# Turning k and x on VectorE in 32x32 blocks instead of on TensorE, with a new order table

## The chip, the cores and the metric

One core of one Trainium2 chip runs the whole program. The metric is device time in microseconds, the median of the runs. The engines are named as in the profile: PE (matmuls; PEld is its weight load), DVE (VectorE), ACT (ScalarE), POOL (GpSimd), and SP, which issues the DMAs.

## The reference

A recurrence with decay (RWKV style) over 4 samples, 8 heads, 768 steps, head size 48, and then a token mix and a feed-forward block of 384 to 1536 to 384 channels:

```python
for t in range(S):
    kt, vt, rt, wt = (k[:, :, t], v[:, :, t], r[:, :, t], w[:, :, t])
    cur = np.einsum('bhd,bhe->bhde', u[None] * kt, vt)
    y[:, :, t] = np.einsum('bhd,bhde->bhe', rt, state + cur)
    state = wt[:, :, :, None] * state + np.einsum('bhd,bhe->bhde', kt, vt)
...
h = xt @ U @ V                        # xt: channels by time, U and V of rank 32
u = x + h.transpose(0, 2, 1)
ch = np.maximum(u @ w_ch1, 0.0) @ w_ch2
return (u + ch).astype(np.float32)
```

## The kernel before

**Chunks.** Time is cut into chunks of 128 steps, six for a sample, 24 in all (chunk g = 6 x sample + chunk). A chunk lies on 128 partitions as channels (two heads of 48, at partitions 0 and 64) by 4 pairs of heads by 128 steps. Its work, with the step names that the order uses: loads of w, r with k, k and r once more in natural order, and v (LW, LRK, LKR, LV on SP); a pass over w that watches its range (GUARD on ACT); two scans of the decay (F and Q on DVE, a reciprocal R between them, the totals T); r and k scaled by them (RP, KS on DVE or POOL); the diagonal from r, k and u (RK, RU, RED) laid into a matrix (SEL, SEL2 on ACT or POOL); the scores (AM on PE) merged into that matrix (CP, a predicated copy on DVE); the output from within the chunk (YA on PE) and from the state (YZ on PE); the state's update (DS on PE; ZA and ZM add and decay it).

**Two turns.** DS contracts over time, so it needs the scaled k with time on partitions. PE turns it: KT, four transposes of 128x128 (L482) into a PSUM bank (tag tr), and ACT copies them to SBUF as kn (KN, L486). The last chunk of a sample updates no state, so 20 chunks are turned. The output y is copied to the tile xT, channels by time (XE, L598); the token mix contracts over time, so x is turned in the same way: XT, three transposes (L616), and XN on ACT (L620), for all 24 chunks. GA on PE takes xn.

**Token mix and feed-forward.** For a sample, GA, G4, SELM, GS and GSL make the rank-32 mix, HP adds it to x (UADD on DVE), and u is split into a high and a low half (UH, UL). Each half sample (384 steps) has twelve up groups of nine matmuls (UP b.h.f, L738; b the sample, h the half), each followed by HH (relu, ACT or DVE) and HL (the low half, DVE, L751), and three outputs of four down groups (DN b.h.c.part, L774), then O (DVE) and OUT (SP). UP, DN and HP share three PSUM buffers: HL, O or UADD frees one. The weights of the feed-forward are split early in the run by ACT, DVE and POOL.

**Order.** Every step is recorded first, then issued in the order of a written-out table (ORDER): a step's number, and whether it runs on its other engine (alt) and how many warming matmuls lead it. Each engine works off its own instructions strictly in that order, and waits on semaphores for the others. After the table's steps come a few rows that check that the decays stayed in range (per, cnt, low, flag); a scheduler puts them among the others, as soon as their inputs are there.

Of the kernel before, what the change touches and what calls it, by code (L numbers as in the profile page):

```python
# [37 lines left out]
def channel_order():
# [19 lines left out]
    "05J05f14y10V04b05L00r05+00Y04z04c05G14+06218Y08o05V00p10W06304-08P05K06001705g18y01905k05-"
    "00a01A00t05O05h11B00u00X15P06405w08x00v05005l08p01C05Q05100w06511y05R05M05p05N02x05S08Z15m06618R06E08Q00H05q"
    "05n08z00x06708T01D09F05r00J08a11+05s08U05t02z05o09E08V00K06801E00Z00L069i8b09N00M09O06A08q08c02N06B00N18d19h"  # L60
    "00b06C80O10c08r06D02y06F00d06G08s02+08+16H82-02P08W16I03008g46J09P08-"
    "06K08t03108h09019q06O06S08e09Q02E03206T08k4A709116P00e06L09R06M02W08u08l0AG06Q08f06N19g06U08m06R12G08i08v08n"
# [924 lines left out]
```

## Time and profile before

| | |
|---|---|
| median of 3 runs | 483.46 us (481.89 to 484.27) |
| profiled execution | 483.14 us, its span 481.4 us |
| mean granted clock of TensorE | 0.976 |
| PE, DVE, ACT, POOL busy | 449.4, 314.6, 171.2, 119.9 us |
| transposes of k on PE (L482) | 80, copies on ACT (L486) 20 of 594 ns |
| transposes of x on PE (L616) | 72, copies on ACT (L620) 24 of 487 ns |

The span runs from the first to the last instruction of the profiled execution; its own time is 1.7 us more. Shares of busy time are means over stages with different limits. Matmul and DVE records overlap with the next one of the same engine, so the time that an instruction takes of its engine is read from its start to the next start where the engine does not wait.

### The profile page before, as it was taken

Reading aid. Unit: us, or ns where it says so; the run is one execution under the profiler, and the core shown is the slowest. Engines: PE = TensorE matmul, PEld = TensorE weight load, DVE = VectorE, ACT = ScalarE, POOL = GpSimd, SP = SyncE. Lnnn points to the kernel's source line nnn. Section 1 sums busy time; section 2 is a strip of 40 time slices with the busy share of each in tenths; the row PEclk is TensorE's granted clock in tenths of the full one; section 3 lists DMA queues with packets and bytes.
Section 4 is the critical chain, followed back from the end, with each engine's and each line's share of the span. In section 5 each row is a group of like instructions: output and inputs, shape, how many; then the busy total and the mean of one; then the engine's idle time right before and its main releaser. Section 6 shows DMA issues by size and latency. Waiting matters only on the chain.

```text
span 481.4 us, 9783 instructions
## 1 busy us (share of the span) xinstructions
PE 449.4 (93%) x4041; PEld 409.8 (85%) x4041; DVE 314.6 (65%) x532; ACT 171.2 (36%) x446; POOL 119.9 (25%) x113
## 2 busy tenths in 40 slices
PE   7568797899999999999999999999999999999994
PEld 3357655799889889899999889799999899999994
DVE  8998999997999888967139558954134144422420
ACT  5485967874524532432044451320011121001000
POOL 3515422534643664402006050600000010000000
PEclk9786999999999999999999999999999999999999
DMA  8653867344105873214024360200000000000001
GB/s 301 226 193 93 298 212 252 116 146 157 38 23 154 251 216 90 75 43 130 18 83 149 100 218 34 84 20 1 33 18 0 19 17 18 0 34 16 1 17 39
DMA packets 20644, 47.38 MB, mean 98 GB/s; under 512 B 2480, under 2 KB 8880, under 8 KB 20592
## 3 DMA queue, kind: packets, MB, share of 16 engines
q1 hardware_dynamic: 20592, 46.67, 30.3%
q8 instruction: 34, 0.56, 0.5%
q14 instruction: 18, 0.15, 0.1%
HBM read 41.94 MB, written 4.72 MB: 97 GB/s over the span
## 4 chain that ended last, share of the span: by engine, by line
PE 70%; DVE 16%; DMA 5%; ACT 4%; issue 3%; POOL 1%; SPq 0%; ACTq 0%; DVEq 0%; POOLq 0%
PE f L774 29%; PE f L738 28%; PE aps L495 3%; DVE F L367 3%; DVE A L498 2%; DMA v<-in_vN 2%; PE y L555 2%; DVE cva_w L297 1%; DMA raw_w<-in_w 1%; PE trk L482 1%; DVE Q L380 1%; PE y L565 1%; PE trx L616 1%; DMA rk<-in_rkT 1%; DVE cva_w L283 1%
## 5 line engine op out<-in xcount | busy, mean ns | idle before, releaser
L738 PE MATMUL f<-u,w1h 128*128 128x384 f32 x576 | 157.0, 343 | 1.6 <-DVE u L705 0.8
L738 PEld LDWEIGHTS f<-u,w1h 128*128 128x128 f32 x576 | 105.3, 188 | 4.5 <-DVE u L705 1.5
L774 PE MATMUL f<-hh,w2h 128*128 128x384 f32 x288 | 99.4, 345 | 0.7 <-DVE hl L751 0.5
L774 PE MATMUL f<-hh,w2l 128*128 128x384 f32 x288 | 97.7, 339 | 0.7 <-POOL w2l L321 0.7
L738 PE MATMUL f<-u,w1l 128*128 128x384 f32 x288 | 97.5, 338 | 0.0
L751 DVE SCALAR_TENSOR_TENSOR hl<-f,hh 128x384 fp32r<-128x384 f32 x96 | 52.7, 552 | 34.9 <-ACT hh L745 33.7
L745 ACT ACTIVATE hh<-f 128x384 fp32r<-128x384 f32 x52 | 25.2, 486 | 137.6 <-PE f L738 137.5
L774 PE MATMUL f<-hl,w2h 128*128 128x384 f32 x288 | 66.7, 339 | 0.1
L774 PEld LDWEIGHTS f<-hh,w2h 128*128 128x128 f32 x288 | 54.1, 188 | 3.0 <-issue 1.0
L774 PEld LDWEIGHTS f<-hh,w2l 128*128 128x128 f32 x288 | 54.1, 188 | 1.2 <-POOL w2l L321 1.0
L738 PEld LDWEIGHTS f<-u,w1l 128*128 128x128 f32 x288 | 54.1, 188 | 0.0
L774 PEld LDWEIGHTS f<-hl,w2h 128*128 128x128 f32 x288 | 51.9, 188 | 0.5 <-DVE hl L751 0.4
L789 DVE TENSOR_TENSOR xT<-f,xT 128x384 f32<-128x384 f32 x24 | 13.3, 554 | 50.7 <-PE f L774 50.6
L747 DVE TENSOR_SCALAR hh<-f 128x384 fp32r<-128x384 f32 x44 | 24.2, 552 | 31.0 <-PE f L738 30.7
L430 ACT ACTIVATE A<-ident,dv 128x128 f32<-128x128 f32 x112 | 35.6, 392 | 24.8 <-PE y L565 16.1
L498 DVE COPY_PREDICATED A<-maskf,aps 128x1024 f32<-128x1024 uint32 x24 | 31.5, 1313 | 11.4 <-PE aps L495 5.7
L304 POOL TENSOR_TENSOR cva_w<-cva_w,raw_w 128x384 int32<-128x384 int32 x24 | 28.3, 1182 | 42.1 <-DVE cva_w L297 16.7
L432 POOL TENSOR_SCALAR_AFFINE_SELECT A<-dv 128x512 f32<-128x512 f32 x20 | 15.9, 804 | 75.5 <-PE y L565 58.9
L367 DVE TENSOR_TENSOR_SCAN F<-w,resets 128x517 f32<-128x517 f32 x24 | 33.4, 1399 | 1.8 <-POOL rk L392 1.3
L495 PE MATMUL aps<-rk 48*128 48x128 f32 x384 | 29.7, 297 | 3.8 <-DVE A L498 2.9
L380 DVE TENSOR_TENSOR_SCAN Q<-w,qd 128x516 f32<-128x516 f32 x24 | 32.5, 1354 | 0.1
L495 PEld LDWEIGHTS aps<-rk 48*128 48x128 f32 x384 | 25.0, 199 | 8.8 <-issue 3.7
(116 smaller groups left out, 575.7 us busy)
## 6 DMA issues: line engine op xcount, KB each, us to landing
rk<-in_rkT SPq DMA_DIRECT2D x24, 512.0 KB, 4.4
raw_w<-in_w SPq DMA_DIRECT2D x24, 384.0 KB, 4.2
kr<-in_rkN SPq DMA_DIRECT2D x18, 384.0 KB, 3.9
w<-in_wT SPq DMA_DIRECT2D x24, 258.5 KB, 2.8
v<-in_vN SPq DMA_DIRECT2D x24, 224.0 KB, 3.3
out_dram<-xT SPq DMA_DIRECT2D x24, 192.0 KB, 1.9
raw_V<-in_V SPq DMA_DIRECT2D x6, 96.0 KB, 4.2
raw_U<-in_U SPq DMA_DIRECT2D x1, 192.0 KB, 4.3
```

The costliest lines, as they stand in the source:

```text
L304: lambda: nc.gpsimd.tensor_tensor(out=d["to"].bitcast(I32), in0=d["a"].bitcast(I32), in1=d["e"], op=ALU.add),
L367: nc.vector.tensor_tensor_scan(out=F[:, ::-1], data0=st["w"][:, ::-1], data1=resets[:, ::-1], initial=1.0, op0=ALU.mult, op1=ALU.add)
L380: nc.vector.tensor_tensor_scan(out=st["Q"], data0=st["w"][:, 0:n], data1=qd, initial=0.0, op0=ALU.mult, op1=ALU.add)
L430: nc.scalar.activation(A[:, i, j], ident, AF.Copy, scale=dv[:, NP * i + j : NP * i + j + 1])
L432: nc.gpsimd.affine_select(out=A[:, i], in_=dv[:, NP * i : NP * i + NP].unsqueeze(2).broadcast_to([P, NP, P]), pattern=[[0, NP], [1, P]], c ...
L495: nc.tensor.matmul(aps[:, i, j, :], rk[r, 1, j, :], rk[r, 0, j, :], start=True, stop=True)
L498: nc.vector.copy_predicated(flat(st["A"]), mask8, flat(st["aps"]))
L738: nc.tensor.matmul(ps, wt[:, f, ct, :], u[ct][:, z], start=(n == 0), stop=(n == 8))
L745: nc.scalar.activation(hh, d["ps", f], AF.Relu)
L747: nc.vector.tensor_scalar(out=hh, in0=d["ps", f], scalar1=0.0, scalar2=None, op0=ALU.max)
L751: nc.vector.scalar_tensor_tensor(out=hl, in0=d["ps", f], scalar=0.0, in1=hh.bitcast(F32), op0=ALU.max, op1=ALU.subtract)
L774: nc.tensor.matmul(d["o", ct], wt[:, 4 * ct + part, f - 3 * part, :], hid[f][z], start=(part == 0 and n == 0), stop=(part == 3 and n == 8),)
```

## The change

For chunks 12 to 23 the turn of k, and for chunks 18 to 23 the turn of x, is made by DVE: a transpose there turns blocks of 32x32, so a chunk takes 16 instructions in four steps (KD or XD) of four, each from 32 partitions to 32 partitions. PE's transposes and ACT's copies of these chunks go. The table is written anew.

```diff
+TURN_K_DVE, TURN_X_DVE = range(12, 24), range(18, 24)
...
 ORDER = (
-    "3n01g01F03p00004C01X03s03r04E03y03u03o03t03v01h01i04D01j01G04d01k00104e01I00201l01H05304F04L03q01Z01J04H01m0"
+    "3n03p01g01F00004C01X03s03r04E03y03u03o03v04D01h01i04e01j01G05301k00101I01H01l04d00204F04L03t13q01Z01J04H01m0"
...
+        def turn_k_blocks(i):
+            if i == 0:
+                st["kn"] = sb2.tile([P, NP, P], F32, tag="kn", name=f"kn_{g}")
+            turn_blocks(st["kn"], st["rk"][:, 1], i)
...
         if on:
-            btr = Buf("tr")
-            kt = step("KT " + nm, "PE", turn_k, [ks], take=[btr, buf["kn"]], use=[buf["rk"]])
-            kn = step("KN " + nm, "ACT", copy_k, [kt], use=[buf["kn"], btr])
+            if g in TURN_K_DVE:
+                kn = ks
+                for i in range(4):
+                    kn = step(
+                        "KD " + nm, "DVE", lambda i=i: turn_k_blocks(i), [kn], take=[buf["kn"]] if i == 0 else [],
+                        use=[buf["rk"], buf["kn"]],
+                    )
+            else:
+                btr = Buf("tr")
+                kt = step("KT " + nm, "PE", turn_k, [ks], take=[btr, buf["kn"]], use=[buf["rk"]])
+                kn = step("KN " + nm, "ACT", copy_k, [kt], use=[buf["kn"], btr])
...
+    def turn_blocks(to, src, i):
+
+        for j in range(4):
+            nc.vector.transpose(
+                to[32 * j : 32 * j + 32, :, 32 * i : 32 * i + 32], src[32 * i : 32 * i + 32, :, 32 * j : 32 * j + 32]
+            )
...
+        def blocks_of_x(i):
+            if i == 0:
+                d["xn"] = sb2.tile([P, NCT, P], F32, tag="xn", name=f"xn_{b}_{c}", bufs=NCH)
+            turn_blocks(d["xn"], blocks[b, blk][:, :, cc * P : (cc + 1) * P], i)
+
+        if b != "g" and b * NCH + c in TURN_X_DVE:
+            last = after
+            for i in range(4):
+                last = [step(
+                    f"XD {b}.{c}", "DVE", lambda i=i: blocks_of_x(i), last, take=[bxn] if i == 0 else [], use=[bx, bxn],
+                )]
+            d["steps"] = last
+            return
```

Counted over the whole table, DVE has 40 KD and 24 XD steps more, PE 10 KT and 6 XT less, ACT 10 KN and 6 XN less. Steps with a choice of engine moved as well: eight HH from DVE to ACT; four RK and five RU from POOL to DVE; four UL from DVE to POOL; three T from DVE to ACT; two HI from ACT to DVE; one KS to DVE, one ZM to ACT; three SEL2 from POOL to ACT and one SEL back.

On PE, at the last down output but one of sample 1's second half (f_1_1_1), a turn of chunk 20's k (trk) stood between two down groups before:

```order
L774 MATMUL f_1_1_0_2926<-hl_1_10_3258,w2h 128x384
L774 MATMUL f_1_1_0_2926<-hl_1_11_3424,w2h 128x384
L482 MATMUL trk_3465<-ident,rk_3303 128x128 x4
L774 MATMUL f_1_1_1_3472<-hh_1_0_2886,w2h 128x384
L774 MATMUL f_1_1_1_3472<-hh_1_0_2886,w2l 128x384
```

At the same two groups now (L809 is the down matmul, hp the mix for sample 2, y an output, dS a state update, aps scores):

```order
L809 MATMUL f_1_1_0_3463<-hl_1_11_3476,w2h 128x384
L725 MATMUL hp_1_0_3529<-Vst,gs_3458 128x384
L725 MATMUL hp_1_1_3533<-Vst,gs_3458 128x384
L570 MATMUL y_3535<-A_3230,v_3235 32x128 x8
L580 MATMUL y_3535<-A_3230,v_3235 32x128 x8
L512 MATMUL dS<-v_3300,kn_3165 48x48 x8
L502 MATMUL aps_3570<-rk_3045 128x128 x8
L725 MATMUL hp_1_2_3592<-Vst,gs_3458 128x384
L809 MATMUL f_1_1_1_3596<-hh_1_0_3102,w2h 128x384
```

The turn is gone, and the mix of sample 2 and chunk 18's and 19's work, which stood behind all down groups of sample 1, now stand between them.

On DVE, around the low half of sample 2's mix (gs), before:

```order
L789 TENSOR_TENSOR xT_1_2026<-f_1_1_1_3472,xT_1_2026 128x384
L403 RECIPROCAL qd<-F_3512 128x4
L387 TENSOR_TENSOR rk_3373<-rk_3373,Q_3534 128x512
L380 SCALAR_TENSOR_TENSOR Q_3559<-w_3448,qd 128x516
L789 TENSOR_TENSOR xT_1_2026<-f_1_1_2_3536,xT_1_2026 128x384
L660 TENSOR_TENSOR gs_3591<-gb_3579,gs_3591 32x384
L498 COPY_PREDICATED A_3357<-maskf,aps_3582 128x1024
L694 TENSOR_TENSOR xT_0_2596<-hp_0_1_3606,xT_0_2596 128x384
```

And now, where chunk 20's k is turned in four fours (kn from rk, L625), with the check row per<-guard among them:

```order
L625 STREAM_TRANSPOSE kn_3441<-rk_3251 32x4x32 x4
L505 COPY_PREDICATED A_3230<-maskf,aps_3428 128x1024
L695 TENSOR_TENSOR gs_3458<-gb_3439,gs_3458 32x384
L552 TENSOR_TENSOR Z_3473<-dS,tots 128x384
L944 TENSOR_REDUCE per<-guard 128x1
L782 TENSOR_SCALAR hh_1_11_3475<-f_1_1_11_3448 128x384
L625 STREAM_TRANSPOSE kn_3441<-rk_3251 32x4x32 x4
L946 TENSOR_SCALAR per<-per 128x1
L786 SCALAR_TENSOR_TENSOR hl_1_11_3476<-f_1_1_11_3448,hh_1_11_3475 128x384
L625 STREAM_TRANSPOSE kn_3441<-rk_3251 32x4x32 x4
L729 TENSOR_TENSOR xT_0_2487<-hp_0_1_3498,xT_0_2487 128x384
L625 STREAM_TRANSPOSE kn_3441<-rk_3251 32x4x32 x4
```

The mix now comes before sample 1's last up group is worked off (hh and hl of group 11), and sixteen transposes stand between rows of the feed-forward and the mix.

The turns of sample 3's first chunk (18), before on PE, among chunk 18's and 19's other work:

```order
L565 MATMUL y_3643<-A_3357,v_3359 32x128 x8
L616 MATMUL trx_0_3664<-ident,xT_0_3625 128x128 x3
L578 MATMUL y_3643<-rk_3082,Z_3392 32x128 x8
L582 MATMUL y_3643<-rk_3082,Z_3392 32x128 x4
L495 MATMUL aps_3688<-rk_3323 128x128 x8
```

Now on DVE, between the low halves of sample 2's first up groups:

```order
L625 STREAM_TRANSPOSE xn_0_3769<-xT_0_3766 32x3x32 x4
L415 TENSOR_TENSOR kr_3735<-kr_3735 128x384
L786 SCALAR_TENSOR_TENSOR hl_0_2_3785<-f_2_0_2_3752,hh_0_2_3784 128x384
L625 STREAM_TRANSPOSE xn_0_3769<-xT_0_3766 32x3x32 x4
L786 SCALAR_TENSOR_TENSOR hl_0_3_3805<-f_2_0_3_3774,hh_0_3_3804 128x384
L625 STREAM_TRANSPOSE xn_0_3769<-xT_0_3766 32x3x32 x4
L786 SCALAR_TENSOR_TENSOR hl_0_4_3823<-f_2_0_4_3794,hh_0_4_3822 128x384
L625 STREAM_TRANSPOSE xn_0_3769<-xT_0_3766 32x3x32 x4
```

More of the change, by code (lines that the diff above doesn't have):

```diff
@@ L58 @@
[L58 to L62, printed above, removed]
@@ new lines @@
+    "04605U01c05B04R01104g04711204h10I04n14S05504N04l15610A04501d04V04O04P11300P04s04i04W04Q11e10h04j04804t01f15T"
+    "04X14k04o05704f00B04905801400i04T00R00C05u00j05W04p05c04A04w00k04q15X05C10l05d14B04r10m05D01515Y05914U06100Q"
+    "05A05E04u05b00n05H04v00D00o00q04Y05I00S00E01605Z05i00T08O05a05400s00U04Z05j05x05J01805v04a04x05F05y15z05e08X"
+    "00F04y10V05L05f14b00r05+04z00Y04c05G14+06218Y05V08o00p10W06308P05K05-14-"
+    "01705g18y01905k06010a01A00t05O05h11B00u00X15P05w06408x00v05005l08p01C05Q05100w06512x05M05R05p05N01y05S08Z15m"
@@ new lines @@
+    "06618R06E08Q00H05q05n08z00x06708T01D09F00J05r05o02z05s08U05t01+08a19E08V00K06801E00Z00L069g9N08b00M09O06A08q"
+    "08c02N06B00N18d19h00b06C80O10c08r06D02y06F00d06G02+08s08+16H82-02P08W16I03008g46J09P08-"
+    "06K08t03108h09019q06O06S08e09Q02E03206T08k4A709116P00e06L09R06M02W08u08l0AG06Q08f06R19g06U08m06N12G08i06V18n"
+    "08v06W00f09G08j13310g18w12F02O00y12Y02H02Q01z02I06Z09S12R02J01-"
+    "02S06X02009T16c06Y02K06a19p02T06b03D06f06d02L11p02U02106e02M06i06g12202X06h03F06l02Z02302o02V16j02413E02a01r"
@@ new lines @@
+    "08D0B00C20B10E81B30Da0B20B708E0B40B80Ec08F0E91E008I0Ed1E11EA0E50Ee0F308G08J0FX0B518H0ED0B90B60C50C90BA18K0C3"
+    "1CA0C40EE08L0F40C60FY0EF0BB0F508M0EG08N0BE0FZ1BC1BH0C71BF0Db0CB0CC1DR0ER0BG0Dc0Dr0DS0D-"
+    "0E20BK0BD0EB1E30EC1EU0BN0Ev0BL0F60E41Ea0BM0DT0I20Dp0BO1EV1DU0EZ0Ds0BP0F20BQ0Dq0Dt1Eh0EJ0BR0BT0BS0Ei0BW0BU0I3"
+    "1Ej0Du0I41Ek0Dv0Ef0ET0EH0Dw0FO0Eg0BV0BX1BZ0Fa0BY0IW0EI0Bc0EK0C81EL0En0Bd0D70BI1Dx0IX1EM0Dy0BJ0IY0Be0EN0Ex0EW"
+    "0Ba1F70Bf0EO0Hv0Eo0F81EX0Bi0Bb0Bg0FN0EY1I50Bh0J00Ey0EP0Bj0Bl0EQ0Bk0Ez1F10E+0FW0Bm0Ep0FQ0Bn0E-"
@@ new lines @@
+    "0FR1Bo0F90J10Hu0J21Br0FA0F00I10Bs0FB0Hx0Bt0FC0Bu0I01Bp0FF0I80Bq0El0Bv0Bx0I90Bw0Em0By0IA0Eq0FV1Hy0FS0Er0IB0Fb"
+    "1FP0CD0IN0FG0Fc0FH1FT0CG0IZ0IM0Hz0FU0JW0Bz0CH1H+0B+0CI0Is0H-1IV0CE1CF0CJ0JX1IP0CM0CK0Iv0IQ1I-"
+    "0IR0FD0IU0CL0Iw1CN1B-"
+    "0CP0FE0C00Ic0Fd0CO0CS0Es0Id0Fe0FI0CT0CU0FJ0I61Hw0Ie0CV0It0FK0IS0I71Ff0If0JM0CW0Fg0Ia0IO0J30Et0Fh0JN0Ix0IT0CY"
+    "0Ib1K00CX0I+0CQ1Eu0CR0Cb0JV0CZ1JP0FL0Cc0Ce0Iy0FM0JQ1Cd0JU0Js0Fi0JR0Cf0Ca0Ch0Fj0Cg0Iz0K11Fk0JS0J-"
+    "0Fl0IE0Ci1Fm0KM0IC0JT0Cj0Fn0J60Jt0Ck0Fo0ID0KV0Fp0Cn0IF0Cl1J70Fq0Co0Cm0J80Fu0Cp0Fv0J90Fy0Cq0Fz0Fr0Jv0Gs0Fs0Gw"
@@ new lines @@
+    "0IG0Fw1Jw1Jx0Ft0Ii0Gx0F+0Iu0Ig0Gt0Fx0Ij0Jc0Ik1G+0J40Ct0Jy0Cu0Jd0J50Ih0Cv0Je0JA0J+1Cw0G-0JB0F-"
+    "1Cz0Gu1Jf0Gv0C+0Gy1Cx0Gz0Cr0Cy0C-"
+    "0Cs0H01KP0H11D00KQ1KR0K21Jz0JY1G00D10JZ0D20KS0KW0G30G11K30G60G40G20IH0G50II0G90G70KX1G80KY0IJ0GC0GA0GB0IK0GF"
+    "0GD0GE0IL0GI0GG0GH0Il0GJ0GK0Im0Ja0JO0GL0In0KN0Jb0Io0KZ0GO0GM0Ip0GN0JF0GP0Iq0JG0K40GQ0JC0Ir0JH0GR0K51Ju0KU1JI"
+    "0GU0GS0K60GX0GT0GV0JJ0Ga0GW0GY0K70Gb0GZ0K80Gc0JK0K90Jg0JL0Gd0Jh0Gg0KT0JD0Ge0Gh0JE0Gf0Gi0Gj0Gm0Gk0Gl0Gn0H20Go"
+    "0H31H40H50H80H61H70Gp0H91HA0HB0Gq0Gr0HE0HC1HD0HH0HF1HG0Jl0HI0HJ0Jm0Ka1HK0Jn0Kb1Jo0HN0HL1Jp0HQ0HO0HM0Jq0HT0HR"
@@ new lines @@
+    "1Jr0KA0HU1HS0Ji0HV0HW0KB0KO0Jj0HP0HZ0Jk1HX0Kc0HY0Ha0Hb0KF0Kd0Kl0KG0KC0KH0Hc0KD0KI0KE1Hd0KJ0KK0He0KL0Ke0Kf0Hf"
+    "0Kg0Kh0Hi0Ki0Hg0Hj0Kj0Hh0Kk0Hk0Km0Hl0Kn0Ko0Hm0Ho0Kp0Hn0Kq0Kr0Kv0Hp0Ks0Kw0Kt1Kx1Kz0Ku0Lt0Hq0K+0Lu0K-"
+    "0Ky1Lv0L00Lx0L-"
+    "0Hr0Ly0M00Lz0Lw1M11L10L+1Hs0M20Ht0L40L20L30L70L50L60LA0L80L90Lb0LB0LC0LD0LG0LE1LF0LJ0LH0LI0Lc0LK1LL0LM0LP0LN"
+    "0LO0LS0LQ0LR0Ld0LT1LU0LV0LY0LW0LX0LZ0La0Le0Lh0Lf0Lg0Li0Lj0Lk0Ln0Ll0Lm0Lo0Lp0Lq0M30Lr0Ls0M60M40M50M90M70M80MC"
+    "0MA0MB0Md0MD0ME0MF0MI0MG0MH0ML0MJ0MK0Me0MM1MN0MO0MR0MP1MQ0MU0MS1MT0Mf0MV0MW0MX0Ma0MY0MZ0Mb0Mc0Mg0Mj0Mh0Mi0Mk"
@@ L99 @@
+    "0Ml0Mm0Mp0Mn0Mo0Mq0Mr0Ms0Mt0Mu0"
 )
```

58 lines of the change are left out of this document (14 added, 44 removed).

## Prediction

> **What bounds the kernel now.** I read the page from the top, the busy shares and the 40 slices first, then the chain that ended last by engine and line, then three stretches of the span.
>
> ```profile
> span 481.4 us, 9783 instructions
> ...
> PE 449.4 (93%) x4041; PEld 409.8 (85%) x4041; DVE 314.6 (65%) x532; ACT 171.2 (36%) x446; POOL 119.9 (25%) x113
> ...
> PE   7568797899999999999999999999999999999994
> ...
> DVE  8998999997999888967139558954134144422420
> ...
> PE 70%; DVE 16%; DMA 5%; ACT 4%; issue 3%; POOL 1%; SPq 0%; ACTq 0%; DVEq 0%; POOLq 0%
> ```
>
> In the first eight slices (about 97 us) DVE is the full engine and PE is not; from the ninth on PE's digits are all 9, and the chain lies on PE for 70% of the span. So work taken from PE counts only behind 97 us, and there it counts in full as long as no other engine takes its place. The candidate is DVE. Three stretches show how near it is; the first begins with the first feed-forward groups, the second at group 6 of sample 0's second half (UP 0.1.6), the third at group 9 of sample 2's first half (UP 2.0.9). The columns are the stretch, its length, and busy us (instructions) of PE, PEld, DVE, ACT and POOL, then clock and DMA.
>
> ```profile
> 98.44:145.87 47.43, 45.97 (x319) 43.24 (x315) 43.77 (x79) 22.75 (x54) 22.77 (x20) 1.00 0.27 84
> 145.87:331.29 185.42, 183.48 (x1928) 169.00 (x1928) 131.16 (x205) 65.49 (x175) 57.37 (x52) 1.00 0.36 108
> 331.29:475.30 144.01, 144.01 (x925) 140.89 (x924) 48.14 (x90) 14.60 (x30) 2.13 (x2) 1.00 0.05 16
> ```
>
> PE waits 1.46, 1.94 and 0 us in them. DVE's work is 95% of PE's in the first, 71% in the second, 33% in the third. The clock is full in all three, so it explains nothing here. What ended PE's longest waits in the first stretch:
>
> ```profile
> PE f L774 <- POOL w2l L321: 0.7, 1, 0.7
> PE f L774 <- DVE hl L751: 0.5, 1, 0.5
> PE f L774 <- DVE xT L694: 0.3, 1, 0.3
> ```
>
> Half of it is a weight still being split (POOL), which happens only there; the other 0.8 us is DVE being late for a feed-forward group.
>
> **What leaves PE.** Ten turns of k (four transposes each: chunks 12 to 16 and 18 to 22) and six of x (three each: chunks 18 to 23). Records of PE overlap, so the price is from start to next start: the first column of the PE timeline.
>
> ```profile
> 283.59 0.60 PE L482 MATMUL trk<-ident,rk 128*128 128x128 f32 x4
> 283.94 0.42 PE L774 MATMUL f<-hh,w2h 128*128 128x384 f32 x1
> 284.20 0.34 PE L774 MATMUL f<-hh,w2l 128*128 128x384 f32 x1
> 284.38 0.34 PE L774 MATMUL f<-hh,w2h 128*128 128x384 f32 x1
> ...
> 361.50 0.49 PE L616 MATMUL trx<-ident,xT 128*128 128x128 f32 x3
> 361.75 0.42 PE L738 MATMUL f<-u,w1h 128*128 128x384 f32 x1
> 362.01 0.34 PE L738 MATMUL f<-u,w1l 128*128 128x384 f32 x1
> ```
>
> A turn of k holds PE for 283.94 - 283.59 = 0.35 us, and the first feed-forward matmul behind it takes 0.26 instead of 0.18: 0.43 us in all. A turn of x: 0.25 + 0.08 = 0.33 us. 10 x 0.43 + 6 x 0.33 = 6.3 us, not the 10 that 58 records of about 0.17 busy us would suggest. The new table mixes the remaining chunk work more finely into the feed-forward groups: from 100 us on PE returns to a feed-forward group from something else 48 times, against 40 before (counted in the two orders); at 0.08 us each that gives back 0.6. Removed: 5.7 us.
>
> **What ACT loses.** The copies out of PSUM go too, ten of k and six of x:
>
> ```profile
> L486 ACT ACTIVATE kn<-trk 128x512 f32<-128x512 f32 x20 | 11.9, 594 | 12.1 <-PE trk L482 12.0
> ...
> L620 ACT ACTIVATE xn<-trx 128x384 f32<-128x384 f32 x24 | 11.7, 487 | 10.3 <-PE trx L616 10.2
> ```
>
> 10 x 0.594 + 6 x 0.487 = 8.9 us, worth nothing by itself (ACT is busy 36%); the new table fills about half of it with eight more first halves of the hidden layer (HH) taken from DVE. The PSUM bank of the turns is also free earlier.
>
> **What DVE gains.** Each turned chunk becomes sixteen transposes of 32 partitions, 128 elements long for k and 96 for x: 160 + 96 instructions. The trace has no such instruction. DVE records end about 0.08 us after the next one has started, so again starts are compared.
>
> ```profile
> 2.54 0.24 DVE L202 TENSOR_REDUCE sel<-ident 128x32 f32<-128x128 f32 x1
> 2.74 0.06 DVE L169 MEMSET resets<- 128x5 f32 x1
> ...
> 162.03 0.54 DVE L420 TENSOR_REDUCE dv<-kr 128x8 f32<-128x384 f32 x1
> 162.49 0.54 DVE L526 TENSOR_TENSOR Z<-dS,Z 128x384 f32<-128x384 f32 x1
> ...
> 163.97 1.32 DVE L498 COPY_PREDICATED A<-maskf,aps 128x1024 f32<-128x1024 uint32 x1
> 165.17 0.67 DVE L416 TENSOR_TENSOR kr<-kr,u_rep 128x384 f32<-128x384 f32 x1
> ...
> 179.22 1.23 DVE L367 TENSOR_TENSOR_SCAN F<-w,resets 128x517 f32<-128x517 f32 x1
> 180.36 1.00 DVE L694 TENSOR_TENSOR xT<-hp,xT 128x384 f32<-128x384 f32 x2
> ...
> 292.32 0.14 DVE L911 TENSOR_SCALAR per<-per 128x1 f32<-128x1 f32 x1
> 292.38 1.22 DVE L380 TENSOR_TENSOR_SCAN Q<-w,qd 128x516 f32<-128x516 f32 x1
> ...
> 304.72 0.35 DVE L701 CAST u<-xT 128x384 fp32r<-128x384 f32 x1
> 304.98 0.55 DVE L526 TENSOR_TENSOR Z<-dS,Z 128x384 f32<-128x384 f32 x1
> ```
>
> 128 elements took 0.20 us (2.54 to 2.74), 384 took 0.46, so an element costs 1.0 ns and 96 elements 0.167 us. From below: the cast did 384 in 0.26, with a fixed 0.06 (292.32) 0.5 ns per element: 0.13 and 0.11 us. From above: the scan did 517 in 1.14, 2.1 ns per element: 0.335 and 0.27 us. I take the middle, 0.20 and 0.167, since the row with the very length of a k block says it. That is 160 x 0.20 + 96 x 0.167 = 48 us more on DVE, for 5.7 less on PE: it pays only where DVE has room.
>
> *Where it lands.* In the new order the second stretch (UP 0.1.6 to UP 2.0.9) holds 144 of the k blocks and 32 of the x blocks: 28.8 + 5.3 = 34.1 us. The other moves there, counted in the two orders, come to about -3 us: three merges of the scores fewer at 1.2 (163.97 to 165.17), two scalings of k on DVE fewer, three u differences and three small rows fewer, nine products of r and k more at 0.46. DVE: 131.2 + 34.1 - 3 = 162 us. PE: 183.5 less ten turns of k and three of x (5.3), plus 0.6, less three scores groups, two down groups and three smaller ones, some 9 us that the new table puts behind the stretch:
>
> ```profile
> 258.66 1.59 PE f L774 x9
> ...
> 270.24 1.09 PE aps L495 x16
> ```
>
> (3 x 1.09 + 2 x 1.59, and 2 to 3 for the rest.) PE: 170. So DVE goes from 71% of PE's work to 95%, just what the first stretch has. What PE waited there is the price: 1.46 of 45.97 us (3.2%), or without the weight split 0.76 (1.7%). On 170 us that is 2.8 to 5.4; I take the middle, 4.1, against 1.94 now: +2.2 us.
>
> *What else waits.* The blocks of one chunk stand in fours between other rows, so a feed-forward row (HL, which frees one of three PSUM buffers) has at most 4 x 0.20 = 0.8 us more ahead of it. The first of each four waits for the scaled k (POOL or DVE) or the copied x (ACT); the state update that needs k stands 10 us or more of PE work behind. The check rows move too: the reduction of the guards now stands ahead of the last HH of sample 1 and waits for the load and ACT's pass of chunk 23; the rows that DVE has to do between the end of chunk 21's scan, which frees the buffer, and that row (four of 0.46, one of 0.6, a merge of 1.2 and four k blocks) are some 4.5 us, the load 2.8 and the pass about 1, so 0 to 1 us. On SP the loads of w for chunks 15 and later stand behind output writes and k/r loads that they preceded; a late one stops DVE at its scan, which cost this:
>
> ```profile
>   DVE F L367: 0.5, 1
> ...
> w<-in_wT SPq DMA_DIRECT2D x24, 258.5 KB, 2.8
> ```
>
> One or two more such waits are 0 to 1 us. Ahead of 97 us a few rows change places at equal work; 0 to 1 us either way. I put these three at nothing and keep 1 us in the range. In the third stretch PE has 144 us of work against 48 plus some 16 of DVE: full cover.
>
> The sum: -5.7 + 2.2 = -3.5 us. The profiled execution took 483.14 us (span 481.4 and 1.7 around it), 0.3 below the median of 483.46: 479.6 us.
>
> **What the skill says.** The Trainium skill, "VectorE: DVE Perf Modes", section "The three transpose paths", gives 311 ns for 128x128 bf16 on VectorE against 390 on TensorE. Here no run shows the first; a record of 0.20 + 0.08 = 0.28 us is what the rows suggest, and by the page's figure, as an estimate, 176 blocks would be 5 us dearer and the sum about 482. The same page, "Rules for kernel authors", gives a 128x128 transpose to TensorE; the next two rivals are what that would mean here.
>
> **Rivals.**
> *DVE fills up, no gain.* The room in the second stretch is 170 - 162 = 8 us, 0.045 us per block. At 0.25 to 0.27 per block DVE is full, and every HL is late by as much as PE was relieved: 481 to 485 us. For it: DVE's slices there were already 5 to 9. Against it: the 0.20 of the reduction.
> *DVE becomes the bound, slower.* From 0.27 per block of k on, DVE's excess exceeds what PE saves. At the scan's price the 176 blocks cost 22 us more, DVE 185 against PE's 170: 185 + 4 against 176.4 now (185.4 less the 9 moved), less 1.0 for the x turns of the last stretch: +11.6, 495 us; 489 where waits hide within. For it: no row here turns data, and a block may have to be filled before it is drained. Against it: the scan's step waits for the step before, a turned element waits for none.
> *The blocks run at two elements per cycle*, as the cast did: 12 us less DVE, 88% of PE's, waits as now: 477 to 478 us; with no wait left at all 475.5.
>
> **How the numbers follow.** Forecast (477.5 to 481.5) 0.48; cheap blocks 0.10; full DVE 0.22; DVE bound 0.20. Half a percent (2.4 us) is what a measurement tells from no change: below 481.0 faster, above 485.9 slower. Faster: 0.41 + 0.10 + 0.02 = 0.53; same: 0.07 + 0.17 = 0.24; slower: 0.03 + 0.20 = 0.23. The range 476.5 to 489 leaves out the upper half of the bound case and the very lowest.
>
> **What would show it.** Right: blocks at starts 0.20 and 0.17 us apart; DVE near 48 us busier; 58 transposes gone from L482 and L616; PE idle between 150 and 320 us at 3 to 5 us, ended by DVE's hl, u or Z rows. Wrong: blocks 0.27 apart or more, or PE's waits there over 8 us.

## The result and the profile after

The changed kernel takes 489.95 us (median of 3 runs, 489.06 to 492.33) against 483.46: ratio 1.0139 [1.0091, 1.0186] (in brackets the 95% interval). Three later comparisons, on other chips, gave 1.0130 [1.0098, 1.0162], 1.0065 [1.0046, 1.0085] and 1.0062 [1.0035, 1.0088]. It is slower, by 0.6 to 1.4%; why the comparisons differ is not known. 479.6 was forecast.

The page of the changed kernel, in the same lines as the page before (span, busy time, slices of PE and DVE, the chain by engine), and its new groups of instructions by shape (busy us and mean ns behind the bar):

```profile
span 490.6 us, 9917 instructions
...
PE 450.0 (92%) x3982; PEld 406.5 (83%) x3982; DVE 382.9 (78%) x784; ACT 169.8 (35%) x451; POOL 109.5 (22%) x105
...
PE   7576896899999989989999999999999999999994
...
DVE  7898999998989999999999999999447654412410
...
PE 45%; DVE 38%; DMA 6%; issue 5%; ACT 2%; POOL 2%; SPq 0%; DVEq 0%; POOLq 0%; ACTq 0%
...
L625 DVE STREAM_TRANSPOSE kn<-rk 32x128 f32<-32x128 f32 x160 | 48.3, 302 | 2.5
```

```profile
L625 DVE STREAM_TRANSPOSE xn<-xT 32x96 f32<-32x96 f32 x96 | 25.9, 270 | 5.8 <-ACT xT L613 4.5
```

DVE's digits, which fell to between 1 and 9 from the 13th slice on, are now nearly all 9 up to the 28th, and the chain, which lay on PE for 70% and on DVE for 16%, now lies 45 and 38. DVE is 68 us busier, and the blocks alone are 48.3 + 25.9 = 74 us, not 48. The three stretches again, between the same groups (columns as before):

```profile
104.33:151.52 47.19, 45.06 (x314) 42.94 (x313) 43.92 (x81) 21.20 (x50) 21.35 (x18) 1.00 0.27 84
151.52:330.87 179.35, 172.55 (x1743) 155.95 (x1742) 173.43 (x376) 57.58 (x159) 45.59 (x45) 1.00 0.36 109
330.87:484.30 153.43, 152.77 (x1055) 147.75 (x1051) 71.31 (x171) 22.06 (x54) 3.34 (x3) 1.00 0.05 18
```

| stretch | before | after | difference | forecast |
|---|---|---|---|---|
| start to UP 0.1.6 | 145.87 | 151.52 | +5.65 | 0 |
| to UP 2.0.9 | 185.42 | 179.35 | -6.07 | -11.3 |
| to the last down group | 144.01 | 153.43 | +9.42 | +8 |
| rest of the span | 6.1 | 6.3 | +0.2 | 0 |

In the second stretch DVE is busy 173.4 of 179.35 us (97%; 162 of 174, or 93%, was forecast) and PE idles 6.8 us (4.1 forecast). Who ends PE's longest waits there (145 to 345 us; total, times, longest):

```profile
PE f L773 <- DVE hl L786: 3.1, 6, 1.3
...
PE dS L512 <- DVE kn L625: 1.1, 2, 1.0
...
PE f L809 <- DVE hl L786: 0.9, 1, 0.9
```

The low half of a feed-forward group, late, as the forecast named it, and twice a turned k. One step of four blocks in DVE's timeline (start, us):

```profile
263.03 1.31 DVE L505 COPY_PREDICATED A<-maskf,aps 128x1024 f32<-128x1024 uint32 x1
264.23 1.24 DVE L625 STREAM_TRANSPOSE kn<-rk 32x128 f32<-32x128 f32 x4
265.50 0.56 DVE L786 SCALAR_TENSOR_TENSOR hl<-f,hh 128x384 fp32r<-128x384 f32 x1
```

Four blocks hold DVE from 264.23 to 265.50: 0.317 us for each, not 0.20. So there are two losses: 5.65 us ahead of UP 0.1.6, where the blocks have not begun, and the blocks' price behind it.

### The profile page after: what moved, and what is told of

It is laid out like the page before. It is cut to its first block, busy times and chain, and to the rows that moved or that the text cites. A ratio compares the mean times of both kernels' runs of the same rounds, so it can differ in the third digit from the quotient of the medians.

```text
span 490.6 us, 9917 instructions
## 1 busy us (share of the span) xinstructions
PE 450.0 (92%) x3982; PEld 406.5 (83%) x3982; DVE 382.9 (78%) x784; ACT 169.8 (35%) x451; POOL 109.5 (22%) x105
## 3 DMA queue, kind: packets, MB, share of 16 engines
HBM read 41.94 MB, written 4.72 MB: 95 GB/s over the span
## 4 chain that ended last, share of the span: by engine, by line
PE 45%; DVE 38%; DMA 6%; issue 5%; ACT 2%; POOL 2%; SPq 0%; DVEq 0%; POOLq 0%; ACTq 0%
PE f L809 21%; PE f L773 19%; DVE kn L625 7%; DVE Q L382 4%; DVE F L369 4%; DVE hl L786 3%; DVE A L505 3%; DMA raw_w<-in_w 3%; DMA kr<-in_rkN 3%; PE aps L502 2%; DVE hh L782 2%; DVE cva_w L299 2%; DVE rk L389 1%; DVE cva_w L285 1%; DVE kr L418 1%
## 5 line engine op out<-in xcount | busy, mean ns | idle before, releaser
L773 PE MATMUL f<-u,w1h 128*128 128x384 f32 x576 | 161.0, 347 | 6.1 <-DVE hl L786 6.0
L773 PEld LDWEIGHTS f<-u,w1h 128*128 128x128 f32 x576 | 106.5, 189 | 11.7 <-DVE hl L786 8.3
L809 PE MATMUL f<-hh,w2h 128*128 128x384 f32 x288 | 99.4, 345 | 0.0
L809 PE MATMUL f<-hh,w2l 128*128 128x384 f32 x288 | 97.7, 339 | 0.9 <-POOL w2l L323 0.9
L780 ACT ACTIVATE hh<-f 128x384 fp32r<-128x384 f32 x60 | 29.2, 488 | 138.7 <-PE f L773 138.6
L809 PE MATMUL f<-hl,w2h 128*128 128x384 f32 x288 | 66.6, 339 | 0.9 <-DVE hl L786 0.9
L809 PEld LDWEIGHTS f<-hh,w2h 128*128 128x128 f32 x288 | 54.0, 188 | 2.7 <-issue 1.0
L809 PEld LDWEIGHTS f<-hh,w2l 128*128 128x128 f32 x288 | 54.1, 188 | 1.5 <-POOL w2l L323 1.2
L809 PEld LDWEIGHTS f<-hl,w2h 128*128 128x128 f32 x288 | 52.0, 188 | 1.2 <-DVE hl L786 1.2
L625 DVE STREAM_TRANSPOSE kn<-rk 32x128 f32<-32x128 f32 x160 | 48.3, 302 | 2.5
L432 ACT ACTIVATE A<-ident,dv 128x128 f32<-128x128 f32 x120 | 38.0, 394 | 24.4 <-PE y L580 11.2
L740 POOL TENSOR_TENSOR u<-xT,u 128x384 fp32r<-128x384 f32 x10 | 10.8, 1085 | 103.8 <-DVE u L736 85.7
L782 DVE TENSOR_SCALAR hh<-f 128x384 fp32r<-128x384 f32 x36 | 19.8, 551 | 15.6 <-PE f L773 15.4
```

The source lines that it names most:

```text
L432: nc.scalar.activation(A[:, i, j], ident, AF.Copy, scale=dv[:, NP * i + j : NP * i + j + 1])
L625: nc.vector.transpose(to[32 * j : 32 * j + 32, :, 32 * i : 32 * i + 32], src[32 * i : 32 * i + 32, :, 32 * j : 32 * j + 32])
L773: nc.tensor.matmul(ps, wt[:, f, ct, :], u[ct][:, z], start=(n == 0), stop=(n == 8))
L780: nc.scalar.activation(hh, d["ps", f], AF.Relu)
L782: nc.vector.tensor_scalar(out=hh, in0=d["ps", f], scalar1=0.0, scalar2=None, op0=ALU.max)
L809: nc.tensor.matmul(d["o", ct], wt[:, 4 * ct + part, f - 3 * part, :], hid[f][z], start=(part == 0 and n == 0), stop=(part == 3 and n == 8),)
```

## The experiments

Ratios are to the kernel before, timed together on the same chip, with 95% intervals. Two kernels timed on one chip can be compared closely; kernels timed on different chips only to about 0.7%, as the four ratios of the changed kernel show. For those the traces serve: the time of UP 0.1.6, and the length of the second stretch.

### Blocks or early rows?

Two theories: the blocks are too dear and fill DVE; or the rows ahead of 97 us, nearly all of which only changed places, cost the time. The first kernel keeps the blocks and takes the former first 686 steps of the table (the same steps in their old order, thirteen of them on their former engine, up to the first block):

```diff
 ORDER = (
-    "3n03p01g01F00004C01X03s03r04E03y03u03o03v04D01h01i04e01j01G05301k0...
+    "3n01g01F03p00004C01X03s03r04E03y03u03o03t03v01h01i04D01j01G04d01k0...
```

> The table's first 686 steps are those of before (both tables have issued the same set of steps by then, none of it a turned chunk), the rest is the new table; blocks on DVE as in the changed kernel. Theory A (two causes: the early rows cost about 4 to 5 us before any block is turned, and the blocks at 0.32 us each make DVE the bound between 150 and 345 us): 484 to 486 us. Theory B (the later part of the new table is at fault, blocks and early rows are hidden): 489 to 490. Theory C (blocks alone; the early lag is swallowed later because DVE sets the pace anyway): 489 to 490.

485.3 us, 1.0016 [0.9999, 1.0033]. The converse keeps the new table and gives all turns back to PE and ACT, at the places of the first block:

```diff
-TURN_K_DVE, TURN_X_DVE = range(12, 24), range(18, 24)
+TURN_K_DVE, TURN_X_DVE = (), ()
```

> The new table with all turns back on PE and ACT (each at the place of its first block step). Theory A: before plus the early 4 to 5 us plus some finer mixing, 487 to 490 us. Theory B: the table costs it all and PE has its 5.7 us back: 493 to 496. Theory C: 483 to 485.

486.61 us, 1.0051 [1.0029, 1.0073], just under theory A's range. Neither half is the whole. Both undone (the former first steps, and all turns on PE and ACT), so that only the later part of the new table is left:

> The first 686 steps of before, the rest from the new table, all turns on PE and ACT. If the early rows and the blocks are all that the changed kernel loses (theory A), this is the kernel before with a slightly finer mix: 482 to 485.5 us. If the early lag in the run with PE turns was partly swallowed and the late table is better than that of before: 480 to 482. If the late table costs by itself (theory B): 487 or more.

483.19 us, 0.9970 [0.9948, 0.9992]: the later order as such is a little better than the former. The early share was then measured directly, the changed kernel and the one with the former early rows on one chip:

> The changed kernel, to stand on one chip beside the one with the former early rows. It measured 1.0139, 1.013 and 1.0065 of the kernel before in three comparisons, each on another chip: between 1.006 and 1.014 again.

> The changed kernel with the former first 686 steps, blocks as changed. If the early rows cost 0.8% whatever the chip (theory E), it stands 0.8 to 1.2% under e17_again; if that figure came from comparing chips (rival), the two stand within 0.4%, and nearly the whole loss is the blocks'.

487.32 us (1.0062 [1.0035, 1.0088]) and 484.82 us (1.0013 [0.9992, 1.0034]): 0.5%, 2.5 us, with an interval of some 0.3% to either side. The rival's bound of 0.4% lies within it, and the other theory's 0.8% at its edge, but the traces show the loss too. In nine profiles with the former early rows UP 0.1.6 begins at 144.5 to 148.3 us, mean 146.25; in eight with the new ones at 147.2 to 151.5, mean 149.5: 3.3 us later. At the mix of sample 0 (SELM) it is already there; PE's timeline of the kernel before, and of the one after:

```profile
72.41 0.87 PE L651 MATMUL gb<-g,sel 128*96 128x384 f32 x2
```

```profile
76.24 0.88 PE L686 MATMUL gb<-g,sel 128*96 128x384 f32 x2
```

Which rows? Chunk 3's product of r and k (PR 3) stands behind two scans (Q 3 and F 4) now and stood ahead of them before; chunk 1's scores (AM 1) begin about 3 us later than before. Each was moved ahead in the changed table, alone and together (shown for PR 3):

```diff
-    "04X14k04o05704f00B04905801400i0...05X05C10l05d14B0...
+    "04X14k04o05704f00B04905C15801400i0...05X00l05d14B0...
```

> The changed kernel with one step moved: the product of r and k for chunk 3 (PR 3 on DVE) stands ahead of the scan Q 3, as before the change, so that POOL's three scalings of 1.2 us or more no longer run beside three two-input DVE rows that took 1.5 to 1.7 us instead of 0.5 to 0.7. If that collision is the early loss: 3 to 4 us less than the changed kernel (486 to 487.5). If the early loss comes from elsewhere (the output products MD 2 ahead of the scores AM 1, loads): within 1 us of it, 489 to 491.

> The changed kernel with one step moved on PE: the scores AM 1 stand ahead of the products MD 2 again, as before the change. In every profile with the new early rows AM 1 began at 33.8 to 34.1 us, in every one with the old rows at 30.7 to 31.7. If that is the lasting part of the early loss (AM 1 late, so the merge and the state behind it): 2 to 3 us less than the changed kernel of the same call. If AM 1 has slack there: within 1 us of it.

> Both moves, AM 1 ahead of MD 2 and PR 3 ahead of Q 3. If they are the early loss: as the run with all 686 early steps of before, 1.0 to 1.2% under the changed kernel of the same call (485 to 486 us). If other rows matter too: 487 to 489.

> The changed kernel again, beside the others, for a narrower interval: 1.012 to 1.015 of before (489 to 491 us). Its profile tells whether the early collision of DVE and POOL rows at 37 to 42 us comes in every execution: AM 2 at 43 us if it does, at 40 to 41 if it fell out the other way.

PR 3: 488.15 us, 1.0064 [1.0040, 1.0089], on another chip than the rest. AM 1: 488.76, 1.0113 [1.0090, 1.0137]; both: 488.85, 1.0108 [1.0084, 1.0132]; neither: 489.39, 1.0130 [1.0098, 1.0162], the three on one chip. The moves win 0.2% at most, and the 1.0064 is no gain either, since the unmoved kernel reads that on two chips.

The traces show one more difference. POOL's scaling of r and k of chunk 3 (RP 3) was released by the scan Q before; now PR 3, behind that scan, releases it. POOL's timeline before and after:

```profile
33.24 1.22 POOL L387 TENSOR_TENSOR rk<-rk,Q 128x512 f32<-128x512 f32 x1 [8.34 <-DVE Q L380]
```

```profile
37.24 1.23 POOL L389 TENSOR_TENSOR rk<-rk,Q 128x512 f32<-128x512 f32 x1 [10.19 <-DVE kr L450]
```

At 37 us it meets DVE's rows with two inputs. DVE's timeline after, from the row that releases POOL:

```profile
36.48 0.68 DVE L450 TENSOR_TENSOR kr<-rk 128x512 f32<-128x512 f32 x1
...
37.35 1.66 DVE L450 TENSOR_TENSOR kr<-rk 128x512 f32<-128x512 f32 x1
38.94 1.53 DVE L299 SCALAR_TENSOR_TENSOR cva_w<-raw_w,cva_w 128x384 uint32<-128x384 uint32 x1
40.39 1.53 DVE L323 TENSOR_TENSOR w1l<-cva_w,w1h 128x384 fp32r<-128x384 f32 x1
```

Three rows that take 0.68, 0.54 and 0.54 us elsewhere take 4.72 together: 3 us of the full engine. Five of the eight profiles with the new early rows show this, and there UP 0.1.6 begins at 150.1 to 151.5 (mean 150.5); in the other three POOL's row is the one that is longer (last section) and it begins at 147.2 to 149.0 (mean 147.9). With the former rows neither happens. So about 2.6 us of the early loss, where it is largest, go with this meeting, and some 1.6 us more have another cause. That is read from profiles: no kernel took the meeting alone away, and moving PR 3, which starts RP 3 at 35.2, only had POOL's row long instead. What the rest is was not found; five of the thirteen steps with another engine stand ahead of the first feed-forward group, and they were not tried by themselves.

### What makes a block dear?

First, the four blocks of a step were replaced by one plain copy of its 32 partitions, which leaves k and x unturned:

```diff
-        for j in range(4):
-            nc.vector.transpose(
-                to[32 * j : 32 * j + 32, :, 32 * i : 32 * i + 32], src[32 * i : 32 * i + 32, :, 32 * j : 32 * j + 32]
-            )
+        nc.vector.tensor_copy(to[32 * i : 32 * i + 32], src[32 * i : 32 * i + 32])
```

> The changed kernel with its own table, but each step of four block transposes is one plain copy of the same 32 partitions (0.3 to 0.4 us instead of 1.26 for k); k and x of those chunks are left unturned. Theory A: DVE has room again and PE's 5.7 us come through, less the early 4 to 5 us: 481 to 484 us. Theory B: 488 to 490. Theory C: 477 to 480.

479.5 us, 0.9883 [0.9855, 0.9911], on the chip of the 1.0016 and 1.0051 above. That is in theory C's range and below A's, though C's claim that the early rows then cost nothing does not fit the pair above. A had the early rows too dear and left the better later order out. With the measured parts it comes out: 1.5 us less by the later order (0.9970), 6.9 less where the turns leave PE (second stretch and the one to the last down group: 174.2 and 154.4 us with all turns on PE, 169.3 and 152.4 here), 2.5 to 3.3 more by the early rows, so 5.1 to 5.9 less, against 5.7 by the ratio. Then by one transpose as long as the four together, which turns k and x within each quarter only, as the third kernel below does too:

```diff
+        nc.vector.transpose(to[32 * i : 32 * i + 32], src[32 * i : 32 * i + 32])
```

> The changed kernel with its own table, but each step is one transpose instruction of 32 partitions by 512 elements (k) or 384 (x) instead of four of 128 or 96: the same elements, a quarter of the instructions; the 32x32 blocks are not put in their other partitions, so k and x of those chunks are turned only within each quarter. If the price of a block is a fixed part of some 0.18 us (no overlap with the next instruction) and 1 ns per element: 0.70 us a step instead of 1.26, DVE 35 us lighter, 479 to 483 us. If it is per element (2.5 ns): 1.3 us a step and 489 to 491 us as the changed kernel.

478.1 us, 0.9878 [0.9832, 0.9925], a little under the range expected. With DVE's time more than the whole loss goes, though the early rows are as changed. Its groups and a piece of its DVE timeline:

```profile
L624 DVE STREAM_TRANSPOSE kn<-rk 32x512 f32<-32x512 f32 x40 | 28.0, 699 | 1.9 <-POOL rk L394 1.1
L624 DVE STREAM_TRANSPOSE xn<-xT 32x384 f32<-32x384 f32 x24 | 13.6, 565 | 7.6 <-ACT xT L613 7.2
```

```profile
169.16 0.70 DVE L624 STREAM_TRANSPOSE kn<-rk 32x512 f32<-32x512 f32 x1 [1.08 <-POOL rk L394]
169.80 0.51 DVE L783 SCALAR_TENSOR_TENSOR hl<-f,hh 128x384 fp32r<-128x384 f32 x1
170.34 2.87 DVE L624 STREAM_TRANSPOSE kn<-rk 32x512 f32<-32x512 f32 x4
...
323.00 0.70 DVE L624 STREAM_TRANSPOSE kn<-rk 32x512 f32<-32x512 f32 x1
323.64 0.53 DVE L624 STREAM_TRANSPOSE xn<-xT 32x384 f32<-32x384 f32 x1
324.18 0.71 DVE L624 STREAM_TRANSPOSE kn<-rk 32x512 f32<-32x512 f32 x1
324.82 0.53 DVE L624 STREAM_TRANSPOSE xn<-xT 32x384 f32<-32x384 f32 x1
```

Here starts and ends say more than means. 169.16 + 0.70 = 169.86, yet the next row starts at 169.80: an overlap of 0.06, as between ordinary rows. This transpose lies on the first 32 partitions, where 128-partition rows begin as well. At 170.34 the third quarter of chunk 12, the second of 13, the fourth of 12 and the third of 13 follow each other: 2.87 us for four records of 0.70, so gaps and no overlap. At 323.00 the third quarters of k and x: overlap 0.06; at 323.64 to 324.18 third to fourth: none; at 324.18 fourth and fourth: 0.07. So it is the change of the quarter of partitions, not the transpose, that lets no row overlap. The plain copies show the same, row by row: those of the first quarter overlap with their neighbours by some 0.07 us where nothing else is waited for, the others leave gaps of 0.01 to 0.03, unless the neighbour lies on the same quarter. The Trainium skill, "VectorE: DVE Perf Modes", section "Two Vector instructions with no wait between them", has this as a rule, which it calls a model: an instruction with an input or an output that begins in another quadrant of 32 partitions than that of the last instruction which read from, or wrote to, the same memory is held until every earlier one has finished. The trace agrees in every pair above.

In the changed kernel each block is written to another quarter than the one before. The test keeps number, size and place of the blocks and takes only that away:

```diff
-                to[32 * j : 32 * j + 32, :, 32 * i : 32 * i + 32], src[32 * i : 32 * i + 32, :, 32 * j : 32 * j + 32]
+                to[32 * i : 32 * i + 32, :, 32 * j : 32 * j + 32], src[32 * i : 32 * i + 32, :, 32 * j : 32 * j + 32]
```

> The changed kernel with the same 256 blocks, of the same size and at the same places of the table, but each block is written to the quarter of partitions that it is read from (k and x of those chunks are turned within quarters only). Theory Q: a DVE row overlaps its forerunner only if it begins at the same one of the four quarters of 32 partitions; then inside a step of four only the first block is held (and not even that in the first quarter). Blocks of k start 0.302 - 0.065 = 0.235 to 0.24 us apart inside a step instead of 0.316, the three gaps of a step save 0.24 us, 64 steps 15 us of DVE; half of what the one long transpose saves (0.53 a step, -2.5%), so a ratio to the kernel before of about 1.000 to 1.006. Rival T: a transpose as such never overlaps; starts stay 0.316 apart and the ratio stays at 1.013.

> The changed kernel once more, to stand beside the one above on the same chip: 1.013 by either theory, blocks 0.316 us apart.

479.6 us, 0.9876 [0.9837, 0.9915], against 488.15 us, 1.0065 [1.0046, 1.0085], for the changed kernel on the same chip (1.013 was expected of that one). The same step of the same chunk in both DVE timelines, first with blocks that stay in their quarter, then as changed:

```profile
168.88 0.87 DVE L625 STREAM_TRANSPOSE kn<-rk 32x128 f32<-32x128 f32 x4
169.69 1.28 DVE L505 COPY_PREDICATED A<-maskf,aps 128x1024 f32<-128x1024 uint32 x1
171.00 0.88 DVE L625 STREAM_TRANSPOSE kn<-rk 32x128 f32<-32x128 f32 x4
171.90 0.56 DVE L418 TENSOR_TENSOR kr<-kr,u_rep 128x384 f32<-128x384 f32 x1
```

```profile
167.87 1.24 DVE L625 STREAM_TRANSPOSE kn<-rk 32x128 f32<-32x128 f32 x4
169.15 1.32 DVE L505 COPY_PREDICATED A<-maskf,aps 128x1024 f32<-128x1024 uint32 x1
170.50 1.25 DVE L625 STREAM_TRANSPOSE kn<-rk 32x128 f32<-32x128 f32 x4
```

0.87 against 1.24. Within a quarter the blocks' records of k are 0.260 us (mean) and overlap by 0.066: 0.193 us from start to start; across quarters 0.302 and a gap of 0.014: 0.316. The change of quarter costs 0.123 us per block. The theory of the quarters holds; its size was foreseen too small (a ratio of 1.000 to 1.006), since a held record is also longer in itself by some 0.043. The test also takes away that a block is read from one quarter and written to another. That is not what makes it dear: here no block does so, and still the first block of a step on the second to fourth quarter, behind a row that begins in another quarter, takes 0.300 to 0.309 us and leaves a gap of 0.013 to 0.032. The second stretch of the two:

```profile
150.06:320.12 170.06, 169.43 (x1743) 155.98 (x1743) 159.42 (x381) 57.35 (x159) 45.66 (x45) 1.00 0.38 115
```

```profile
150.21:327.68 177.47, 172.01 (x1743) 155.84 (x1742) 172.70 (x376) 57.81 (x159) 46.78 (x45) 1.00 0.36 110
```

DVE falls from 97 to 94% of the stretch and PE's idle time from 5.5 to 0.6 us; the stretch is 7.4 us shorter.

### k or x?

With the former early rows and the later part of the new table: x on DVE and k on PE, k on DVE and x on PE, and x with k of three or six of the ten chunks.

```diff
-TURN_K_DVE, TURN_X_DVE = range(12, 24), range(18, 24)
+TURN_K_DVE, TURN_X_DVE = (), range(18, 24)                        # x
+TURN_K_DVE, TURN_X_DVE = range(12, 24), ()                        # k
+TURN_K_DVE, TURN_X_DVE = (18, 20, 22), range(18, 24)              # x, three of k
+TURN_K_DVE, TURN_X_DVE = (12, 14, 16, 18, 20, 22), range(18, 24)  # x, six of k
```

> As the last, but x of chunks 18 to 23 turned on DVE at the new table's places (four blocks at a time between other rows, most of them behind 330 us, where DVE has room). Theory A: 2 us less than the last kernel, as PE loses six turns at 0.33; if groups of four blocks make the low halves late as the sixteen in a row did, 3 us or more above the last.

> First 686 steps of before, the rest from the new table, k of chunks 12 on turned on DVE and x on PE. Theory A (each turn pays or costs by DVE's room where it stands; k fills DVE to 97% between 150 and 300 us): about 1.4 us above the run with both on DVE, 486 to 488 us. If x and k hurt together only (their sum is what fills DVE): 482 to 485.

> The version with x on DVE (481.7 us), plus k of chunks 18, 20 and 22 there at the new table's places: 15 us more on DVE between 200 and 345 us, where it has 41 us free of 145, and 3 x 0.43 us less on PE. Theory A: 0.5 to 1.5 us faster than with x alone, 480 to 481.5. If any k block in the dense part makes low halves late: 482 to 484.

> As the last with k of chunks 12, 14 and 16 too: 30 us of k blocks between 150 and 345 us, DVE at some 85 to 90% there instead of 97. Theory A: the waits that all ten cause (5 us) are mostly gone, 479.5 to 482.5. If waits grow with the number of blocks and not with the room: half of what ten cost, 483 to 484.

x: 481.72 us, 0.9943 [0.9923, 0.9963], the lowest ratio of those that turn k and x in full (three of k beside x is level with it) and faster than both kernels; 0.27% under the one with all turns on PE on the same chip, where the two intervals overlap. k: 484.8, 1.0021 [1.0001, 1.0040], in the range given for the theory that k and x hurt only together; but k and x together, with the same early rows, took no more (1.0016 and 1.0013). Three of k: 481.8, 0.9947 [0.9928, 0.9966]; six: 482.45, 0.9956 [0.9938, 0.9974]. Three of k bring nothing, where a small gain was expected; all of k loses (3 us in the second stretch, below). The stretch from 200 to 300 us shows what changes, for x, x with three, x with six, and k:

```profile
200.00:300.00 100.00, 100.00 (x975) 92.59 (x974) 73.63 (x120) 33.99 (x95) 23.55 (x21) 1.00 0.32 99
```

```profile
200.00:300.00 100.00, 99.59 (x965) 91.57 (x965) 83.14 (x149) 33.97 (x95) 23.56 (x21) 1.00 0.32 101
```

```profile
200.00:300.00 100.00, 97.83 (x950) 89.20 (x949) 87.86 (x167) 30.43 (x86) 22.79 (x21) 1.00 0.31 97
```

```profile
200.00:300.00 100.00, 96.05 (x932) 86.70 (x930) 97.65 (x209) 28.68 (x80) 21.14 (x21) 1.00 0.31 93
```

DVE 74, 83, 88, 98 us; PE idle 0, 0.4, 2.2, 4.0. The busy share alone does not settle it. The whole second stretch of x with six, and of k:

```profile
145.33:320.21 174.88, 172.59 (x1760) 157.57 (x1759) 154.43 (x310) 59.37 (x163) 46.65 (x44) 1.00 0.36 112
```

```profile
144.53:321.93 177.40, 172.29 (x1748) 156.31 (x1747) 165.00 (x345) 58.22 (x161) 45.80 (x44) 1.00 0.36 110
```

Here DVE is 88 and 93% busy and PE idles 2.3 and 5.1 us; with the blocks that stay in their quarter it is 94% busy and PE idles 0.6. PE's longest waits in both are again ended by hl, and a step of four held blocks stands 1.27 us ahead of it, not 0.8 to 0.9; that this is what counts was not tested apart from the share. The second stretch's length, for all kernels from their traces:

| turns in the second stretch | UP 0.1.6 to UP 2.0.9, us |
|---|---|
| all on PE, new table (two kernels) | 174.2, 174.3 |
| x on DVE | 173.6 |
| x and three of k; six of k | 173.9; 174.9 |
| k on DVE | 177.4 |
| k and x on DVE as changed (nine profiles, with moves and former early rows) | 177.0 to 179.4 |
| blocks within a quarter; long transpose; copy | 170.1; 169.6; 169.3 |

One kernel shows what the order of the blocks does: the former table, and x turned at the place of the former turn, all sixteen blocks in a row.

```diff
-TURN_K_DVE, TURN_X_DVE = range(12, 24), range(18, 24)
+TURN_K_DVE, TURN_X_DVE = (), range(18, 24)
...
 ORDER = (    # the former table, each XT/XN replaced by four XD
```

> The table of before with only x of chunks 18 to 23 turned on DVE, sixteen blocks in a row at the place where PE turned it. PE loses 6 x 0.33 = 2 us and DVE gains 96 blocks of 0.28 where it is a third to a half busy. Theory A (room decides): 481 to 482.5 us. If sixteen blocks in a row (4.5 us) make the low halves behind them late, so that PE waits 1 us or more at each: 484 to 489.

506.02 us, 1.0451 [1.0425, 1.0477]. Its DVE timeline and the waits of PE (300 to 345 us):

```profile
303.94 4.50 DVE L619 STREAM_TRANSPOSE xn<-xT 32x96 f32<-32x96 f32 x16
308.45 1.02 DVE L723 TENSOR_TENSOR xT<-hp,xT 128x384 f32<-128x384 f32 x2
```

```profile
PE aps L496 <- DVE A L499: 6.0, 1, 6.0
...
PE dS L506 <- DVE Z L535: 2.9, 1, 2.9
PE f L767 <- DVE u L734: 2.7, 1, 2.7
```

Six times 4.5 us on DVE cost 21.6 us of time: in this order everything that PE needs stands behind the whole turn. Fours between other rows are what makes x cheap in the new table.

## Why the prediction was wrong, by its own steps

**What bounds the kernel now**: right. PE carries the time behind 97 us, DVE is the candidate for the next bound, and it became that.

**What leaves PE** (6.3 less 0.6 us): right. Of the x turns 1.0 us was forecast for the stretch to the last down group; PE works 154.4 us there with all turns on PE and 153.2 with x on DVE. In the second stretch PE is busy 174.1 us with the turns and 169.4 without (blocks within a quarter), 4.7 less where 5.3 was forecast.

**What ACT loses**: worth nothing, as said; ACT stays at 35%.

**What DVE gains**: the term that failed. The 0.20 us was right for a block that is not held (0.193 within a quarter) and left out that each block is held for its change of quarter: 0.316 for k, 0.283 for x. The rows from which the price was worked out all begin at partition 0, so none of them could show it; one row of the profile before, gs, lies on 32 partitions from the 64th on, and it did:

```profile
74.39 0.55 DVE L297 SCALAR_TENSOR_TENSOR cva_w<-raw_w,cva_w 128x384 uint32<-128x384 uint32 x1
74.96 0.56 DVE L660 TENSOR_TENSOR gs<-gb,gs 32x384 fp32r<-32x384 f32 x1
75.55 0.55 DVE L420 TENSOR_REDUCE dv<-kr 128x8 f32<-128x384 f32 x1
```

74.39 + 0.55 = 74.94 and 74.96 + 0.56 = 75.52: a gap ahead of it and one behind it, where other rows overlap by 0.08. 144 blocks of k and 28 of x in the second stretch (32 were counted) are 172 x 0.116 = 20 us dearer. DVE's busy time there is only 11 us above the forecast 162, mostly because gaps are not busy time and because the other moves took off 7.3 us, not 3 (131.2 before, 123.8 in the new table with all turns on PE).

**Where it lands**: 95% of PE's work was forecast; DVE's work came out above PE's own (173.4 against 172.6 us). The stretch is 177.0 to 179.4 us in the profiles, 174.1 forecast: 3 to 5 of the missing microseconds. Had the block been 0.20, the step would have been too dark: with blocks of 0.193 DVE has 94% of PE's work, and PE idled 0.6 us, not 4.1. That the kernel with such blocks takes 479.6 us, the forecast to the digit, is luck: its second stretch is 4.0 us shorter than forecast and UP 0.1.6 comes 4.2 later.

**What else waits**: the early rows, put at 0 to 1 us and at nothing in the sum, cost 3.3 by the traces and 2.5 by the timed pair. That they hold equal work was nearly true (up to UP 0.1.6 DVE is busy 133.4 to 135.3 us with the former rows, 134.5 to 135.1 with the new ones where the meeting did not slow it) and did not bound the cost: ahead of 97 us DVE is full, and a POOL row that starts 4 us later met it there. The check rows and the loads of w were rightly put at nothing: PE's list of waits shows mostly hl and kn. The full cover forecast for the last 144 us of PE's work failed by one wait of 0.6 us for hl.

**The sum**: 479.6 plus 3.3 early, 3 to 5 in the second stretch and 1.4 in the one behind it (9.4 against 8: that wait of 0.6, and 0.8 more work) is 487.3 to 489.3, where the kernel measured 487.3 to 490.0. Of the signs of being wrong, blocks 0.27 us apart or more came true; PE's waits over 8 us did not (6.8).

**The rivals**: "DVE becomes the bound", from 0.27 us per block on, is what happened (DVE's slices in the second stretch, given for the rival before it as 5 to 9, were 1 to 9); its 489 us "where waits hide within" is near the result, partly by chance, since 3 us of it are the early rows'. Its argument, a block filled before it is drained, is not the cause: a transpose within a quarter takes 0.193 us, no more than the reduction of that length. The cheap blocks, two elements per cycle, are refuted: four times the length adds 0.699 - 0.302 = 0.397 us to a record, 1.03 ns per element, as forecast.

**What the Trainium skill says**: the 311 ns that the Trainium skill, "VectorE: DVE Perf Modes", section "The three transpose paths", gives for a 128x128 bf16 on VectorE came closer to the block's record (0.302 us) than the 0.28 taken from the rows, though it is for another shape and type. The estimate of 482 made with it fell short for the same reasons as the sum: it still let each block overlap with the next, and it had the early rows at nothing; how 5 us of DVE became 2.4 of time was not worked out there. The rule of the Trainium skill, "VectorE: DVE Perf Modes", section "Rules for kernel authors", that gives a 128x128 transpose to TensorE holds here for k; for x, where DVE has room, the measurements show no loss and perhaps a small gain.

## What to carry to other kernels

Price a DVE instruction on a part of the partitions by its neighbours as well: if it begins in another quarter than the row ahead, it does not overlap, and here 0.20 became 0.316 us. Moving work from a full engine to one at 70% pays only while that one still delivers in time, and its busy share alone does not tell: here PE idled 0.6 us with DVE at 94% and short steps, 5.1 at 93% with long ones and 5 to 7 at 97%. An error of a tenth of a microsecond on 176 instructions helped to turn the sign. Rows that only change places are free only where their engine has idle time; where it is full, a reordering needs a measurement of its own.
